# Layer norm of the four plain groups: statistics tile by tile, and ScalarE in place of VectorE for the normalisation

## The chip, the core and the metric

The kernel runs on one core of a Trainium2 chip. A core has TensorE (matrix products, results in PSUM), VectorE, ScalarE and GpSimd (element-wise work), and queues that start DMA transfers. Each engine works through its own queue in order; an instruction that waits for another engine holds up all that stands behind it in its queue. The metric is the time of one execution on the device in microseconds (us).

## What is computed

Two blocks in a row, all in float32. First a linear attention with decay over 4 batches, 8 heads, 768 positions and 64 columns per head, in blocks. Its result x, 4 x 768 x 512, goes through a Fourier mixing block:

```python
X = np.fft.fft(np.fft.fft(x, axis=1), axis=2)
u = x + np.real(X).astype(np.float32)
mu = np.mean(u, axis=-1, keepdims=True)
var = np.mean((u - mu) ** 2, axis=-1, keepdims=True)
un = (u - mu) / np.sqrt(var + 1e-06)
ch = np.maximum(un @ w_ch1, 0.0) @ w_ch2
return u + ch
```

Here w_ch1 is 512 x 2048 and w_ch2 is 2048 x 512. They arrive as float64 and are turned into float32 on the chip (`load_weights`, L203). The change is in the lines of `un`: the mean, the variance and the normalisation.

## The kernel before

**Tiles and groups.** A batch has six tiles of 128 tokens (partitions) by 512 columns. The Fourier transform gives tile t and tile 3 + t together, since the one is the mirror of the other, so a *group* (b, g) is the pair of tiles (g, 3 + g) of batch b, and there are 12 groups, worked through in the order g = 1, 2, 0 of each batch. The first four in that order, (0,1), (0,2), (0,0) and (1,1), are called PLAIN: their MLP is done with ordinary matrix products (`mlp`, L711), beside the attention and the Fourier transforms of the later batches, and fills TensorE while these wait. The other eight, LATE, are written to DRAM and go through a second stage with Strassen-like products (from `late`, L1246), in which fewer multiplications are needed.

**One group in `fft_ln` (L572).** For each t in (1, 2, 0) the width product runs on TensorE (`width`, L605) into one bank of PSUM; ScalarE copies parts of it (L674 to L677); VectorE forms `ds` (L678, L679) and adds it to the two tiles of the group, `u` (L681) and `v_` (L682). For t = 0 one row of `v_` is replaced (L688 to L691). Then `norm(g)` (L622) is called:

- L626 and L627, VectorE: `bn_stats` and `bn_aggr` of each of the two tiles give mean and variance, in `mv`.
- L630 and L631, GpSimd: `ve` = variance + epsilon, `rs` = `ve` to the power -0.5, both tiles in one instruction.
- L644, VectorE: `un` = (x - mean) * power, in two halves per tile, the second half read backwards. `un` has a single buffer (`bufs=1`).
- In a plain group: L649, TensorE transposes the four blocks of `un` into PSUM, and L653, ScalarE copies them into `ut`, which the MLP's first layer reads (L718). In a late group: VectorE transposes in blocks (L657) and the result goes to DRAM (L661).

The plain MLP evicts the first layer's results from three PSUM banks (`pm`) with a Relu on ScalarE, L726, in the second half also on VectorE, L724; its second layer is L732.

**What orders the work.** The Python generators (`weave`, `beside`, `part`) decide in which order instructions are written down, by the costs that they yield (`yield 9.0`, `yield 1.6` and so on). The order of each engine's queue is then fixed at build time by a planner, which plays the program through with its own estimates of durations and puts the earliest-written instruction that it takes to be ready at each engine's turn. So a queue's order is not the program's order, but once built it doesn't change. `tc.keep_in_program_order` pins an instruction behind the one written before it on its engine; the first transpose of the first plain group is pinned in this way. Semaphores between engines are set by the framework.

**GpSimd's queue** also carries the gathers of mirrored rows (L483, L489, L496), and the products `kd` (L304) and state decays (L356) of the attention.

Of the kernel before, what the change touches and what calls it, by code (L numbers as in the profile page):

```python
# [16 lines left out]
AF = mybir.ActivationFunctionType  # L17
ALU = mybir.AluOpType
# [59 lines left out]
def kernel(  # L78
# [10 lines left out]
    nc = tc.nc  # L89
# [14 lines left out]
    G = 2  # L104
    NG = NC // G
    TT = [(t, HC + t) for t in range(HC)]
# [9 lines left out]
    def front_pool(name, bufs):  # L116
        return front_end.enter_context(tc.tile_pool(name=name, bufs=bufs, side="left"))
# [9 lines left out]
    np_ = front_pool("np", 2)  # L127
# [12 lines left out]
    def new(pool, shape, tag, **kw):  # L140
        cnt[0] += 1
        return pool.tile(shape, F32, tag=tag, name=f"{tag}{cnt[0]}", **kw)

    def psum_a(shape):
        return new(pa, shape, "pa")
# [28 lines left out]
    mhalf = const.tile([128, G], F32, name="mhalf")  # L174
# [100 lines left out]
    xs, xn_, xd = {}, {}, {}  # L275
# [224 lines left out]
    def fold_a(b):  # L500
        for a, n in enumerate(BLK):
            yield from fold_x(b, a, n, 1, eo[b][a][1][0:n, 1, 0:DM], xn_[b, HC + a][0:n])
# [69 lines left out]
    def fft_ln(b):  # L572
        sets = []

        def piece(a, i, n):

            c0 = W + QM if i == 4 else QM * (i % 2)
            return sets[a][i in (2, 3)][0:BLK[a], n, c0:c0 + QM]

        if b in LEADS:  # L580
            yield from fold_a(b)
            yield from fold_b(b, sets)
            yield 2.0
        else:
            yield 1.0
            run(fold_a(b))
            yield 6.0 if b - 1 in LEADS else 3.0
            run((folds_apart if b > 1 else fold_b)(b, sets))
            yield 12.0 if b - 1 in LEADS else 9.0


        for i in (0, 1, 4, 2, 3):
            ps = psum_a([128, 2, NK])
            m = 128 if i < 4 else 1
            for n in range(2):
                for a, rows in enumerate(BLK):
                    mm = nc.tensor.matmul(ps[:, n, :], lhsT=piece(a, i, n), rhs=cs[0:rows, a, i in (2, 3), n, :],  # L597
                                          start=(a == 0), stop=(a == 1))
                    if i + n + a == 0:
                        tc.keep_in_program_order(mm)  # L600
            nc.scalar.copy(ys[i][0:m, 0:2 * NK].rearrange("p (k n) -> p n k", n=2), ps[0:m])
            yield 1.4


        def width(t, ps, only_a):  # L605
            y = [ys[i][:, S // 2:S // 2 + 1].broadcast_to([128, 128]) if only_a else ys[i][:, 128 * t:128 * t + 128] for i in range(5)]
            mm = nc.tensor.matmul
            if not only_a:
                mm(ps[:, HM + QM:DM], lhsT=y[2], rhs=dt[:, 2, 0:QM], start=True, stop=True)
            mm(ps[:, HM:HM + QM + 1], lhsT=y[0], rhs=dt[:, 0, :], start=True, stop=False)  # L610
            mm(ps[:, HM:HM + QM + 1], lhsT=y[4], rhs=dt[:, 4, :], start=False, stop=True)
            mm(ps[:, 0:QM], lhsT=y[1], rhs=dt[:, 1, 0:QM], start=True, stop=True)
            if not only_a:
                mm(ps[:, QM:HM], lhsT=y[3], rhs=dt[:, 3, 0:QM], start=True, stop=True)

        def even_odd(t):
            return t.rearrange("p (m r) -> p r m", r=2)

        def halves(t):
            return t.rearrange("p (r k) -> p r k", r=2)  # L620

        def norm(g):  # L622
            mv = new(np_, [128, G, 2], "mv")
            for i in range(G):
                stt = new(np_, [128, 6], "stt")
                nc.vector.bn_stats(stt, xs[b, TT[g][i]])  # L626
                nc.vector.bn_aggr(mv[:, i, :], stt)  # L627
            ve = new(np_, [128, G], "ve")
            rs = new(np_, [128, G], "rs")
            nc.gpsimd.tensor_scalar(ve, mv[:, :, 1], EPS, None, op0=ALU.add)  # L630
            nc.gpsimd.tensor_tensor(rs, ve, mhalf, op=ALU.pow)  # L631

            yield 9.0 if (b, g) == PLAIN[0] else 1.0
            plain = (b, g) in PLAIN
            if plain:
                ut = uts[b, g] = new(up, [128, KO, G * 128], "ut")
            else:

                to = utd[b, g] = dram.tile([128, KO, G * 128], F32, name=f"utd{b}{g}")
            for i in range(G):  # L640
                un = new(np_, [128, DM], "un", bufs=1)
                u = xs[b, TT[g][i]]
                for o, x in ((un[:, 0:HM], u[:, 0:HM]), (un[:, HM:DM], u[:, DM - 1:HM - 1:-1])):
                    nc.vector.tensor_scalar(o, x, mv[:, i, 0:1], rs[:, i:i + 1],  # L644
                                            op0=ALU.subtract, op1=ALU.mult)
                if plain:
                    pt = psum_a([128, KO, 128])
                    for c in range(KO):
                        mm = nc.tensor.transpose(pt[:, c, :], un[:, 128 * c:128 * c + 128], ident)  # L649
                        if (b, g, i, c) == (*PLAIN[0], 0, 0):  # L650

                            tc.keep_in_program_order(mm)
                    nc.scalar.copy(ut[:, :, 128 * i:128 * i + 128], pt)  # L653
                else:

                    uq = new(ep, [128, DM], "e")
                    nc.vector.transpose(uq, un)  # L657
                    for r in range(0, 128, 32):
                        dst = to[:, :, 128 * i + r:128 * i + r + 32].rearrange("(a d) c n -> d c a n", d=32)
                        src = uq[r:r + 32].rearrange("p (c a n) -> p c a n", c=KO, n=32)  # L660
                        nc.sync.dma_start(dst, src)  # L661
                yield 0.7
            if plain:
                return
            for T in TT[g]:
                ud[b, T] = dram.tile([128, DM], F32, name=f"ud{b}{T}")
                nc.sync.dma_start(ud[b, T], xs.pop((b, T)))

        for t in (1, 2, 0):
            ps = psum_a([128, DM])  # L670
            width(t, ps, False)

            A = halves(ps)[:, ::-1, 0:QM]
            nc.scalar.copy(odd[:, 1:HM:2], ps[:, QM:HM])  # L674
            nc.scalar.copy(odd[:, 2:HM:2], ps[:, HM + QM + 1:DM])
            ds = new(fp, [128, 2 * (HM + 2)], "ds")
            nc.scalar.copy(ds[:, HM:2 * HM + 2:HM + 1], ps[:, HM + QM:HM + QM + 1].broadcast_to([128, 2]))  # L677
            nc.vector.tensor_tensor(even_odd(ds[:, 0:HM]), A, even_odd(odd[:, :]), op=ALU.subtract)  # L678
            nc.vector.tensor_tensor(even_odd(ds[:, HM + 1:2 * HM + 1]), A, even_odd(odd[:, :]), op=ALU.add)  # L679
            u, v_ = xs[b, t], xs[b, HC + t]  # L680
            nc.vector.tensor_tensor(halves(u), halves(u), halves(ds)[:, :, 0:HM], op=ALU.add)  # L681
            nc.vector.tensor_tensor(halves(v_), halves(v_), halves(ds[:, 1:DM + 1])[:, ::-1, :], op=ALU.add)  # L682
            yield 1.6
            if t == 0:
                ps = psum_a([128, DM])
                width(HC, ps, True)
                x3 = xn_.pop((b, HC))
                nc.vector.tensor_tensor(even_odd(v_[0:1, 0:HM]), halves(ps[0:1])[:, ::-1, 0:QM],  # L688
                                        even_odd(x3[0:1, 0:HM]), op=ALU.add)
                nc.vector.tensor_tensor(v_[0:1, HM:DM:2], ps[0:1, 0:QM], x3[0:1, HM:DM:2], op=ALU.add)  # L690
                nc.vector.tensor_tensor(v_[0:1, HM + 1:DM:2], ps[0:1, HM + 1:HM + QM + 1],  # L691
                                        x3[0:1, HM + 1:DM:2], op=ALU.add)
                yield 0.9
            yield from norm(t)


    ORDER = [(b, g) for b in range(B) for g in (1, 2, 0)]
    PLAIN, LATE = ORDER[:4], ORDER[4:]
# [565 lines left out]
    def front(b):  # L1264
        yield from attn(b)
        yield from fft_ln(b)
# [15 lines left out]
    def run(gen):  # L1282
        return sum(gen)
# [18 lines left out]
    def beside(lead, t, other, t_other):  # L1302
        return weave(lead, part(other, t_other), t_other / t)

    att1, mix = attn(1), fft_ln(0)
    att0 = attn(0)
    run(part(att0, 2.7))
# [4 lines left out]

    half = [[mlp(b, g, h * FO // 2, (h + 1) * FO // 2) for b, g in PLAIN[:3]] for h in range(2)]
    fr = chain([att1, fft_ln(1)] + [front(b) for b in range(2, B)])
    t_rest, t_back = 3 * t_front - 5 * t_chunk, len(PLAIN) * t_mlp - 50.0
    t_half = 1.5 * t_mlp
# [49 lines left out]
```

## Time and profile before

| | |
|---|---|
| median of 3 runs | 785.93 us (785.44 to 786.23) |
| the profiled execution | 782.96 us |
| its span, first to last instruction | 780.7 us |
| TensorE busy | 756.3 us |
| VectorE busy | 600.9 us |
| ScalarE busy | 231.9 us |
| GpSimd busy | 181.9 us |
| TensorE's granted clock | 1.00 |
| L644, normalisation, 48 instructions | 0.41 us each |
| L631, power, 12 instructions | 0.72 us each |
| first to last transpose of a plain `un` (L649) | 92.4 to 148.4 us |

A line of the profile names the engine (PE is TensorE, PEld its weight loads, DVE VectorE, ACT ScalarE, POOL GpSimd), the line of the kernel, the operation and the tiles as out<-in. Times are counted from the span's start. Behind a line may stand in brackets how long the engine was idle before the instruction and which instruction ended the wait. The span is divided into the attention and Fourier stage with the plain MLP (up to some 391 us), and the second stage, in which TensorE runs the late groups.

### The profile page before, as it was taken

Reading aid. Unit: us, or ns where it says so; the run is one execution under the profiler, and the core shown is the slowest. Engines: PE = TensorE matmul, PEld = TensorE weight load, DVE = VectorE, ACT = ScalarE, POOL = GpSimd, SP = SyncE. Lnnn points to the kernel's source line nnn. Section 1 sums busy time; section 2 is a strip of 40 time slices with the busy share of each in tenths; the row PEclk is TensorE's granted clock in tenths of the full one; section 3 lists DMA queues with packets and bytes.
Section 4 is the critical chain, followed back from the end, with each engine's and each line's share of the span. In section 5 each row is a group of like instructions: output and inputs, shape, how many; then the busy total and the mean of one; then the engine's idle time right before and its main releaser. Section 6 shows DMA issues by size and latency. Waiting matters only on the chain.

```text
span 780.7 us, 14995 instructions
## 1 busy us (share of the span) xinstructions
PE 756.3 (97%) x5784; PEld 646.9 (83%) x5784; DVE 600.9 (77%) x1167; ACT 231.9 (30%) x532; POOL 181.9 (23%) x202
## 2 busy tenths in 40 slices
PE   6989989999999999999999999999999999999997
PEld 5768776858676877858946889999999999999997
DVE  6899889675855585346698999789986699758983
ACT  3765443325531221421101221024311342024310
POOL 3223331010202113211003961360015000230013
PEclk9999999999999999999999999999999999999999
DMA  9979623237852148721243374776545455455442
GB/s 241 255 164 249 189 91 122 87 68 202 221 153 89 55 81 250 194 90 41 55 121 102 140 242 137 264 246 194 181 137 162 142 176 178 133 177 175 137 141 75
DMA packets 152955, 120.21 MB, mean 154 GB/s; under 512 B 114238, under 2 KB 114622, under 8 KB 152886
## 3 DMA queue, kind: packets, MB, share of 16 engines
q1 hardware_dynamic: 145824, 100.51, 45.7%
q0 software_dynamic: 4032, 12.99, 4.6%
q10 hardware_dynamic: 3030, 5.78, 2.0%
q8 instruction: 46, 0.75, 0.4%
q14 instruction: 23, 0.19, 0.1%
HBM read 88.04 MB, written 31.20 MB: 153 GB/s over the span
## 4 chain that ended last, share of the span: by engine, by line
PE 85%; DVE 7%; DMA 4%; ACT 2%; issue 1%; POOL 1%; DVEq 0%; ACTq 0%; POOLq 0%
PE p L1127 22%; PE p L1053 17%; PE pm L732 12%; PE pm L718 11%; PE p L969 6%; PE pa L597 3%; PE pa L332 3%; PE pa L373 3%; PE pa L367 2%; DMA x<-xb,ix 2%; PE pa L308 1%; PE pa L352 1%; PE pa L313 1%; PE pa L389 1%; DVE sc L336 1%
## 5 line engine op out<-in xcount | busy, mean ns | idle before, releaser
L718 PE MATMUL pm<-ut,w 128*128 128x256 f32 x512 | 118.3, 381 | 0.0
L732 PE MATMUL pm<-w,hr 128*128 128x512 f32 x256 | 115.3, 596 | 0.1
L718 PEld LDWEIGHTS pm<-ut,w 128*128 128x128 f32 x512 | 94.5, 190 | 13.6 <-issue 2.1
L732 PEld LDWEIGHTS pm<-w,hr 128*128 128x128 f32 x256 | 46.7, 190 | 50.3 <-issue 48.7
L1148 POOL TENSOR_TENSOR y<-y,u 128x512 f32<-128x512 f32 x12 | 19.9, 1660 | 186.8 <-DVE y L1157 155.6
L1127 PE MATMUL p<-tx,sx 128*128 128x128 f32 x400 | 52.7, 275 | 0.0
L1127 PEld LDWEIGHTS p<-tx,sx 128*128 128x128 f32 x400 | 48.6, 192 | 0.0
L1062 DVE TENSOR_TENSOR ha<-p,ha 128x512 f32<-128x512 f32 x60 | 40.1, 686 | 8.3 <-PE p L1053 8.1
L304 POOL TENSOR_TENSOR kd<-k,decay 128x512 f32<-128x512 f32 x20 | 22.9, 1144 | 96.0 <-PE pa L352 56.1
L1133 ACT COPY y<-p 128x128 f32<-128x128 f32 x48 | 12.7, 265 | 103.6 <-PE p L1127 103.2
L1135 DVE TENSOR_TENSOR y<-p,y 128x128 f32<-128x128 f32 x92 | 25.6, 285 | 16.1 <-PE p L1127 9.4
L1127 PE MATMUL p<-w,ha 128*128 128x128 f32 x288 | 37.4, 275 | 0.0
L336 DVE TENSOR_TENSOR sc<-pa,decay 128x512 f32<-128x512 f32 x48 | 31.5, 683 | 7.6 <-PE pa L332 7.3
L332 PEld LDWEIGHTS pa<-qT,kT 64*128 64x128 f32 x384 | 26.1, 193 | 12.8 <-ACT qT L315 7.6
L1062 DVE TENSOR_TENSOR hs<-p,hs 128x512 f32<-128x512 f32 x39 | 26.2, 686 | 12.3 <-PE p L1053 12.3
L726 ACT ACTIVATE hr<-pm 128x256 f32<-128x256 f32 x44 | 16.7, 384 | 63.9 <-PE pm L718 63.7
L1127 PEld LDWEIGHTS p<-w,ha 128*128 128x128 f32 x288 | 34.9, 192 | 0.1
L1053 PE MATMUL p<-sx,tx 128*128 128x128 f32 x264 | 33.9, 275 | 0.0
L332 PE MATMUL pa<-qT,kT 64*128 64x128 f32 x384 | 30.7, 292 | 3.2 <-ACT qT L315 2.9
L319 DVE TENSOR_TENSOR qs<-pa,qpow 128x512 f32<-128x512 f32 x20 | 13.7, 686 | 24.3 <-ACT qT L315 24.2
L373 PE MATMUL pa<-sc,v 128*64 128x128 f32 x384 | 29.9, 279 | 2.0 <-DVE sc L336 1.9
L1053 PEld LDWEIGHTS p<-sx,tx 128*128 128x128 f32 x264 | 31.6, 192 | 0.0
(267 smaller groups left out, 1731.5 us busy)
## 6 DMA issues: line engine op xcount, KB each, us to landing
tx<-td SPq DMA_DIRECT2D x84, 256.0 KB, 2.7
raw<-in_moe_w_ch_dram SPq DMA_DIRECT2D x32, 512.0 KB, 3.7
tx<-sd SPq DMA_DIRECT2D x63, 256.0 KB, 2.8
k<-in_k_dram SPq DMA_DIRECT2D x24, 256.0 KB, 5.7
q<-in_q_dram SPq DMA_DIRECT2D x24, 256.0 KB, 5.9
v<-in_v_dram SPq DMA_DIRECT2D x24, 256.0 KB, 5.1
td<-tx SPq DMA_DIRECT2D x21, 256.0 KB, 2.0
ud<-x SPq DMA_DIRECT2D x16, 256.0 KB, 2.2
```

The source lines that it names most:

```text
L304: nc.gpsimd.tensor_tensor(kd, kt, kpow, op=ALU.mult)
L332: mm(pss[hi][:, hp, :], lhsT=kT[HD[hi], hp, :], rhs=qT[HD[hi], hp, :], start=True, stop=True)
L336: nc.vector.tensor_tensor(t, pss[hi], decay[:, hi::2, :], op=ALU.mult)
L373: mm(po[HD[hi], hp, :], lhsT=vt[:, 2 * hp + hi, :], rhs=sc[hi][:, hp, :], start=(c == 0 and hp == 0), stop=(hp == HP - 1), skip_group_chec ...
L597: mm = nc.tensor.matmul(ps[:, n, :], lhsT=piece(a, i, n), rhs=cs[0:rows, a, i in (2, 3), n, :], start=(a == 0), stop=(a == 1))
L718: nc.tensor.matmul(ps, lhsT=w1[:, c, 128 * fc:128 * fc + 128], rhs=ut[:, c, :], start=(c == 0), stop=(c == KO - 1))
L732: nc.tensor.matmul(ps, lhsT=hr[(fc - f0) // 4][:, fc % 4, 128 * i:128 * i + 128], rhs=w2[:, fc, :], start=(fc == f0), stop=(fc == f1 - 1))
L969: nc.tensor.matmul(ps, lhsT=s2.A[a][:, kt, 128 * i:128 * i + 128], rhs=U[b][:, kt, :], start=(first and kt == 0), stop=(kt == 1), skip_gro ...
L1053: nc.tensor.matmul(ps[:, 128 * i:128 * i + 128], lhsT=ab[m][0][:, 128 * i:128 * i + 128], rhs=ab[m][1], start=(start and i == 0), stop=Tru ...
L1062: V.tensor_tensor(o, p, o, op=ADD)
L1127: nc.tensor.matmul(ps[:, 0:HM // 2], lhsT=ab[m][0][i], rhs=ab[m][1][:, i, :], start=(start and i == 0), stop=(i == HF // 2 - 1), skip_grou ...
L1135: V.tensor_tensor(o, ps[:, 0:HM // 2], o, op=ADD)
```

## The change

In the plain groups each tile gets statistics of its own. For the first tile `u` they are written down directly behind its sum, ahead of the sum of the second tile; GpSimd's two instructions work on one column instead of two. GpSimd then forms `shift` = mean * power * (-1) for each tile, and ScalarE computes `un` as Identity(power * x + shift), with power and shift as one value per partition, in the same two halves. In the late groups the arithmetic and its order stay as they are.

```diff
-        def norm(g):
-            mv = new(np_, [128, G, 2], "mv")
-            for i in range(G):
+        def statistics(tiles, mv, ve, rs):
+            for i, x in enumerate(tiles):
                 stt = new(np_, [128, 6], "stt")
-                nc.vector.bn_stats(stt, xs[b, TT[g][i]])
+                nc.vector.bn_stats(stt, x)
                 nc.vector.bn_aggr(mv[:, i, :], stt)
-            ve = new(np_, [128, G], "ve")
-            rs = new(np_, [128, G], "rs")
             nc.gpsimd.tensor_scalar(ve, mv[:, :, 1], EPS, None, op0=ALU.add)
-            nc.gpsimd.tensor_tensor(rs, ve, mhalf, op=ALU.pow)
-
+            nc.gpsimd.tensor_tensor(rs, ve, mhalf[:, 0:len(tiles)], op=ALU.pow)
+
+        def norm(g, mv, rs):
             yield 9.0 if (b, g) == PLAIN[0] else 1.0
             plain = (b, g) in PLAIN
...
             for i in range(G):
                 un = new(np_, [128, DM], "un", bufs=1)
                 u = xs[b, TT[g][i]]
+                mean, power = mv[:, i, 0:1], rs[:, i:i + 1]
+                if plain:
+                    shift = new(np_, [128, 1], "shift")
+                    nc.gpsimd.tensor_scalar(shift, mean, power, -1.0, op0=ALU.mult, op1=ALU.mult)
                 for o, x in ((un[:, 0:HM], u[:, 0:HM]), (un[:, HM:DM], u[:, DM - 1:HM - 1:-1])):
-                    nc.vector.tensor_scalar(o, x, mv[:, i, 0:1], rs[:, i:i + 1],
-                                            op0=ALU.subtract, op1=ALU.mult)
+                    if plain:
+                        nc.scalar.activation(o, x, AF.Identity, bias=shift, scale=power)
+                    else:
+                        nc.vector.tensor_scalar(o, x, mean, power, op0=ALU.subtract, op1=ALU.mult)
...
             u, v_ = xs[b, t], xs[b, HC + t]
+            each = (b, t) in PLAIN
+            mv, ve, rs = (new(np_, [128, *n], m) for m, n in (("mv", (G, 2)), ("ve", (G,)), ("rs", (G,))))
             nc.vector.tensor_tensor(halves(u), halves(u), halves(ds)[:, :, 0:HM], op=ALU.add)
+            if each:
+                statistics([u], mv[:, 0:1], ve[:, 0:1], rs[:, 0:1])
             nc.vector.tensor_tensor(halves(v_), halves(v_), halves(ds[:, 1:DM + 1])[:, ::-1, :], op=ALU.add)
...
-            yield from norm(t)
+            if each:
+                statistics([v_], mv[:, 1:2], ve[:, 1:2], rs[:, 1:2])
+            else:
+                statistics([u, v_], mv, ve, rs)
+            yield from norm(t, mv, rs)
```

## The prediction

> **What bounds the kernel now.** I read the page's busy shares first, then the busy time by stretch, then TensorE's waits, then the timeline of one group.
>
> ```profile
> PE 756.3 (97%) x5784; PEld 646.9 (83%) x5784; DVE 600.9 (77%) x1167; ACT 231.9 (30%) x532; POOL 181.9 (23%) x202
> ```
>
> TensorE is busy 97% of 780.7 us. An engine that gets lighter elsewhere buys nothing unless TensorE stops waiting for it. The busy time by stretch (columns: length, then PE, PEld, DVE, ACT, POOL, the clock, DMA) shows where TensorE has gaps in the part that the change touches:
>
> ```profile
> 85.00:90.00 5.00, 4.08 (x52) 3.48 (x54) 5.00 (x13) 2.93 (x6) 1.13 (x2) 1.00 0.59 129
> 90.00:95.00 5.00, 4.15 (x45) 3.23 (x42) 3.32 (x8) 1.66 (x3) 2.56 (x4) 1.00 0.77 210
> 95.00:100.00 5.00, 5.00 (x28) 4.25 (x26) 3.47 (x8) 1.36 (x6) 1.93 (x4) 1.00 0.86 312
> 100.00:105.00 5.00, 3.96 (x31) 3.63 (x31) 3.84 (x10) 3.14 (x7) 0.56 (x1) 1.00 0.04 11
> ...
> 110.00:115.00 5.00, 4.06 (x22) 3.02 (x21) 4.08 (x12) 2.31 (x6) 3.27 (x4) 1.00 0.24 71
> ...
> 145.00:150.00 5.00, 4.06 (x28) 3.33 (x27) 1.55 (x5) 0.42 (x2) 0.94 (x2) 1.00 0.00 0
> ```
>
> The gaps are 0.92, 0.85, 1.04, 0.94 and 0.94 us, 4.7 us in all; from 150 to 345 us the same view has PE busy for the whole of every stretch. The waits of TensorE name what ended them (engine, line, waited for: us in total, times, longest):
>
> ```profile
> PE pa L649 <- DVE un L644: 3.4, 4, 1.0
> PE pa L597 <- DVE fe L520: 1.1, 2, 0.7
> PE pa L367 <- DVE qs L319: 0.6, 1, 0.6
> ```
>
> The first line is the transpose of the normalised tile `un`: four waits, 0.51 at 93.59, 1.04 at 101.16, 0.94 at 113.19 and 0.94 at 146.71. That sum of 3.4 us is all that a quicker `un` can give directly. The timeline of the second group, (b, g) = (0, 2), shows the chain (start, duration, what, and in brackets the idle time before it):
>
> ```profile
> 96.73 0.69 DVE L681 TENSOR_TENSOR x<-x,ds 128x512 f32<-128x512 f32 x1
> 97.34 0.68 DVE L682 TENSOR_TENSOR x<-x,ds 128x512 f32<-128x512 f32 x1
> 97.94 1.28 DVE L626 BATCH_NORM_STATS2 stt<-x 128x6 f32<-128x512 f32 x2
> 99.13 0.30 DVE L627 BATCH_NORM_AGGREGATE mv<-stt 128x2 f32<-128x6 f32 x2
> 99.53 0.22 POOL L630 TENSOR_SCALAR ve<-mv 128x2 f32<-128x2 f32 x1 [2.68 <-DVE mv L627]
> 99.83 0.73 POOL L631 TENSOR_TENSOR rs<-ve,mhalf 128x2 f32<-128x2 f32 x1
> 100.60 0.74 DVE L644 TENSOR_SCALAR un<-x,mv,rs 128x256 f32<-128x256 f32 x2 [1.16 <-POOL rs L631]
> 101.16 0.67 PE L649 MATMUL pa<-ident,un 128*128 128x128 f32 x4 [1.04 <-DVE un L644]
> ```
>
> The reader is to see two things. TensorE's queue reached the transpose about 1 us before `un` was there, and by the same 0.94 to 1.04 us in three groups: the order of its queue was fixed at build time on an estimate of this chain that is some 1 us short. And on VectorE both `bn_stats` run before the first `bn_aggr`, although the program writes stats, aggregate, stats, aggregate: work that is ready goes ahead of work that still waits for its input.
>
> **VectorE: sixteen `tensor_scalar` go.** Each lasts 0.41 us (the row L644), 6.5 us in all; with them go the waits in front of them, 3.2 us for `rs` and 1.6 us for TensorE (four plain groups). Beside: TensorE has MLP matmuls in its queue throughout, and only 0.5 us of its other waits here name VectorE's weight conversion (L228, at 128.75). I take 0; the ends are 0 and -0.5 us.
>
> **ScalarE: sixteen Identity activations come.** No row shows one. The nearest: Relu 128x256 from PSUM 0.384 (L726); SBUF as source against PSUM adds 0.045 for 128x512 (L1067 0.631 against L1060 0.586); a bias from SBUF adds at most 0.04 (L221 0.721 against L219 0.688). That makes 0.43 to 0.5 us for a half, 7 to 8 us in all, on an engine that is busy 30%. Sign, Relu and Copy ran on one table load (1.283 us, at the start); I take it that Identity needs no other, and were it otherwise two swaps per group would cost up to 2.6 us each, which I leave out of the range as very unlikely. The first half of `un` would be ready 0.02 to 0.1 us later than VectorE's, given the same start; I take 0.05.
>
> The Trainium skill ("ScalarE: Activation LUTs", What ACT_TABLE_LOAD costs) adds 93 ns for each [128,1] pointer operand to 186 + 0.833 N ns; two of them at N = 256 make an estimate of 0.585 us, where the row with one pointer shows a good deal less than that addition; by the page the sum below would be 0.1 us higher per group, 0.4 in all. Its rule that plain adds and multiplies belong on VectorE speaks against the change, and no run here shows it for two pointers.
>
> The ScalarE instruction now waits for `shift`. Queued behind it are the Relu evictions L726 that free the three `pm` banks (one per 1.73 us of L718), the copies of `ut`, and the copies L674 to L677 of the next width product. A hold-up of 1 us is less than the 2 x 1.73 us that the other two banks cover: 0.
>
> **GpSimd: two tiny instructions per group become six.** `ve` costs 0.22 (0.58 when VectorE is dense), `rs` 0.72 for two columns; for one column I have only bounds, 0.36 (half) to 0.72. `shift` is like `ve`, 0.22 to 0.58. POOL is 23% busy; the row transfers (L496) of the next batch stand behind them at 112.7 and move by 0.3 to 1 us, behind VectorE work that fills 115 to 137 us: 0.
>
> **The chain to TensorE, group by group.**
> - (0,2) and (1,1). By the order seen on VectorE (a ready instruction first), L682 and both `bn_stats` still run before the first `bn_aggr`, so the tile's own statistics gain 0.13 us (99.30 against 99.43). Then on POOL, with the gaps of the timeline (0.08 between dependent instructions): `ve` of the first tile to 99.61, `ve` of the second to 99.87, `rs` 99.90 to 100.26 or 100.62, `shift` to 100.56 or 100.92, first half of `un` 0.45 later, TensorE 0.15 after it: 101.20 to 101.56, against 101.16 now. If the second tile's `rs` stands ahead of the first's `shift`, 0.36 to 0.72 more, up to 102.28. So +0.04 to +1.1 us for TensorE, if its queue keeps its order. The planner of the queue sees the longer chain too and puts MLP matmuls in front (0.43 us apiece), which takes back about half. I take +0.5 for each of the two, +1.0.
> - (0,0). Here the row-0 repairs L688 to L691 part the tiles: the first `bn_aggr` is at 109.61, the second at 110.93. The first tile's chain starts 1.3 us sooner: `ve` 109.87, `rs` 110.2 to 110.9, `shift` 111.2, `un` 111.7, ready 112.0 where TensorE comes free at 112.25. The wait of 0.94 can go entirely, or stay, if the planner draws the transpose forward by as much. I take -0.7.
> - (0,1). `un` was ready at 92.27, before TensorE (92.49); the new chain has 0.8 us of slack there, since VectorE did other work between `rs` (91.04) and `un` (91.86): 0.
> - Second tiles. `un` has one buffer, so the second tile waits for the first's transposes, as now. On ScalarE the copy of `ut` (0.585) becomes ready at the same moment and may go first: 0.585 + 0.45 + 0.15 = 1.2 us until the next transpose, against 0.86 to 1.03 of matmuls that lie between now. 0 to 0.2 each, 0 to 0.8 in all; against it the 0.51 of (0,1) may go. I take +0.2.
>
> Sum: 0 + 0 + 0 + 1.0 - 0.7 + 0 + 0.2 = **+0.5 us**. From 150 us TensorE is full, so a delay before it reaches the end undiminished. The profiled execution took 782.96 (span 780.7 and 2.3 around it), so it would be 783.5; the runs' median is 785.93, 2.97 above it, and I predict **786.4**.
>
> **The rivals.**
> *Faster*: the four waits of 3.4 us go and nothing takes their place. It needs the first tile's statistics to run ahead of L682, and `shift` right behind its own `rs`. For it: the chain of waits runs through exactly these instructions, and VectorE's queue loses 11 us between 84 and 150. Against: a ready instruction is placed before a dependent one wherever the trace lets me look. -3.4 + 0.4 left = -3.0: 782.9. Chance 0.27.
> *Slower*: GpSimd's queue has the second tile's `rs` ahead of the first's `shift`, and the planner does not know how long `rs` is. For it: `bn_stats` passes `bn_aggr` in this way, and the waits of 1 us show an estimate that is short on this chain. Against: `rs` of the second tile waits for its own `ve`. +1.1 in (0,2) and in (1,1), +0.8 at the second tiles, no gain in (0,0): +3.0, 788.9. It decides from the point where the pair costs over 0.6 us more than planned. Chance 0.36, with a new order of the whole queue after 90 us counted in, which can add about what the gap at 350 to 360 us has now (1.0 us) once more.
> *The change doesn't do what it says*: statistics apart are of no use if both tiles' come out within 0.15 us, as in three of four groups. This is part of my forecast.
>
> **The numbers.** Forecast (within 0.2%, 1.6 us, about what a measurement of this kernel tells from no change): 0.37; faster 0.27; slower 0.36. Range: all four waits gone, 782.5, to the slower rival with a new gap of 1.0, 789.9. I give **782.5 to 789.9**.
>
> **What would show it.** In the changed profile: L649's waits for `un` (now on ACT) near 3.4 us or above means the forecast, under 1 us the faster rival, over 5 us the slower. POOL's order in the group after 96 us decides about `rs` and `shift`. VectorE's order there decides whether statistics came sooner. An activation of over 0.6 us, a second table load, or new gaps of TensorE after 150 us would make the prediction wrong.

## The result, and the profile after

The changed kernel takes 796.60 us (median of 6 runs, 796.09 to 799.46); the kernel before, run beside it, 785.68 us (6 runs, 783.34 to 786.77). The ratio is 1.0151 with an interval of 1.0127 to 1.0175: 1.5% slower, outside the range of the prediction. The profiled execution took 796.48 us, with a span of 794.7, 14.0 us longer than the span before; the medians differ by 10.9, since the profiled execution before lies 2.7 us under its median here.

The busy times of the changed kernel:

```profile
PE 761.0 (96%) x5784; PEld 651.4 (82%) x5784; DVE 597.5 (75%) x1151; ACT 239.1 (30%) x548; POOL 186.4 (23%) x218
```

VectorE and ScalarE moved as the diff says (16 instructions fewer, 16 more). TensorE runs the same 5784 instructions, yet is busy 4.7 us longer. The waits of TensorE, then ScalarE, then VectorE (engine, tile and line, what ended the wait: us in total, times, longest). In the changed kernel `un` of a plain group is L647, its transpose L653, `shift` L644:

```profile
PE pa L653 <- ACT un L647: 11.8, 4, 5.4
```

```profile
ACT un L647 <- POOL shift L644: 14.3, 4, 5.6
```

```profile
DVE e L223 <- ACT e L221: 14.8, 5, 6.7
```

TensorE's waits for `un` grew from 3.4 to 11.8 us. With +8.4 of waits and +4.7 of busy time, 13.1 of the 14.0 us are named. Some 1.0 us of the 14.0 is there ahead of the plain groups: the products of L367 that begin at 83.87 us before begin at 84.88, and up to there the engines run the same instructions in the same order in both kernels, so it isn't the change's. Of the four waits for `un`, three (3.33, 5.41 and 1.84 us) end with ScalarE's own wait for GpSimd's `shift`. The fourth, 1.17 us at the second tile of (0,1), does not: there ScalarE was still at the copies of L376 and L657 when the buffer of `un` came free. In the kernel before, VectorE had this row in the stretch of 84 to 165 us:

```profile
DVE un L644 <- POOL rs L631: 4.1, 4, 1.2
```

Three of these four stops, 3.2 us, are in plain groups; the last, 0.84 us at 157.16, is in the late group (1,2), whose code is as before. After the change VectorE never stops for GpSimd in a plain group. Where it waits most now, it is for ScalarE's weight conversion (L221), which stands in ScalarE's queue behind the `un` that waits.

The timeline of the changed kernel's third group, (0,0), is where the largest wait lies (start, duration, what, in brackets the idle time before it):

```profile
117.38 4.71 POOL L644 TENSOR_SCALAR shift<-mv,rs 128x1 f32<-128x1 f32 x1
117.39 0.16 DVE L626 BATCH_NORM_AGGREGATE mv<-stt 128x2 f32<-128x6 f32 x1
117.48 0.65 DVE L470 TENSOR_TENSOR fe<-fo,xn 65x512 f32<-65x512 f32 x1
118.06 0.41 DVE L223 TENSOR_TENSOR e<-e 128x512 bf16<-128x512 bf16 x1
...
120.94 0.41 DVE L220 TENSOR_SCALAR e<-raw 128x512 uint16<-128x512 uint16 x1
121.27 0.67 DVE L227 SCALAR_TENSOR_TENSOR w<-raw,w 128x512 f32<-128x512 uint32 x1
122.12 0.60 ACT L647 ACTIVATE un<-x,shift,rs 128x256 f32<-128x256 f32 x1 [5.63 <-POOL shift L644]
...
122.77 0.69 PE L653 MATMUL pa<-ident,un 128*128 128x128 f32 x2 [5.41 <-ACT un L647]
```

The reader is to see that one instruction on 128 numbers takes 4.71 us, that VectorE works without a gap all that time (six more VectorE instructions stand where lines are left out, each starting before the one ahead of it has drained), and that `shift` ends at 122.09, 0.15 us after VectorE's last instruction (121.27 + 0.67 = 121.94) has ended and its queue paused. ScalarE, which waits for `shift`, starts 0.03 us behind that, so a second engine bears out the end of this long instruction. The group (0,2) shows the same in small:

```profile
101.55 0.72 POOL L627 TENSOR_SCALAR ve<-mv 128x1 f32<-128x1 f32 x1 [3.79 <-DVE mv L626]
...
102.36 1.32 POOL L628 TENSOR_TENSOR rs<-ve,mhalf 128x1 f32<-128x1 f32 x1
...
103.76 0.68 POOL L627 TENSOR_SCALAR ve<-mv 128x1 f32<-128x1 f32 x1
104.53 0.57 POOL L628 TENSOR_TENSOR rs<-ve,mhalf 128x1 f32<-128x1 f32 x1
105.08 0.51 POOL L644 TENSOR_SCALAR shift<-mv,rs 128x1 f32<-128x1 f32 x2
...
106.05 1.18 PE L653 MATMUL pa<-ident,un 128*128 128x128 f32 x4 [3.33 <-ACT un L647]
```

The first three GpSimd instructions, beside VectorE's weight conversion (101.51 to 104.36), are stretched; the later ones, when VectorE has nothing to do, last 0.57 and 0.26 each. It also shows GpSimd's order: the second tile's `ve` and `rs` stand ahead of the first tile's `shift`.

Last, the busy time of the changed kernel by stretch, around and behind the waits that end at 106.05, 122.77 and 159.59 (columns: length, PE, PEld, DVE, ACT, POOL, the granted clock, DMA):

```profile
106.00:108.00 2.00, 1.95 (x7) 1.57 (x8) 0.00 (x0) 1.78 (x4) 0.00 (x0) 0.50 0.04 8
...
120.00:122.00 2.00, 0.00 (x0) 0.00 (x0) 1.95 (x5) 0.00 (x0) 2.00 (x1) 1.00 0.00 0
122.00:124.00 2.00, 1.23 (x4) 1.14 (x5) 0.00 (x0) 1.63 (x4) 1.14 (x4) 0.70 0.01 4
124.00:126.00 2.00, 2.00 (x7) 1.53 (x7) 0.00 (x0) 0.76 (x2) 0.43 (x1) 0.50 0.35 131
...
160.00:162.00 2.00, 1.95 (x7) 1.52 (x7) 0.00 (x0) 1.38 (x4) 0.00 (x0) 0.58 0.00 0
```

Behind each of the three waits (3.33, 5.41 and 1.84 us) the clock is half for some 3.4 us. Half of 3.4 is lost, three times: 5.1 us, about the 4.7 by which TensorE is busier. So the changed kernel pays for a long wait twice.

### The profile page after: what moved, and what is told of

It is laid out like the page before. It is cut to its first block, busy times and chain, and to the rows that moved or that the text cites. A ratio compares the mean times of both kernels' runs of the same rounds, so it can differ in the third digit from the quotient of the medians.

```text
span 794.7 us, 15023 instructions
## 1 busy us (share of the span) xinstructions
PE 761.0 (96%) x5784; PEld 651.4 (82%) x5784; DVE 597.5 (75%) x1151; ACT 239.1 (30%) x548; POOL 186.4 (23%) x218
## 4 chain that ended last, share of the span: by engine, by line
PE 66%; POOL 5%; issue 5%; DMA 2%; DVE 1%; SPq 0%; ACT 0%; POOLq 0%; DVEq 0%
PE p L1139 17%; PE p L1065 17%; PE pm L744 12%; PE pm L730 11%; POOL tx L817 3%; PE pa L332 2%; PE pa L597 2%; PE pa L373 1%; PE pa L367 1%; DMA ur<-utd 1%; PE pa L352 1%; PE pa L308 1%; PE pa L389 1%; PE pa L313 1%; POOL w L813 1%
## 5 line engine op out<-in xcount | busy, mean ns | idle before, releaser
L730 PE MATMUL pm<-ut,w 128*128 128x256 f32 x512 | 121.5, 388 | 0.0
L730 PEld LDWEIGHTS pm<-ut,w 128*128 128x128 f32 x512 | 96.7, 195 | 13.8 <-issue 1.6
L336 DVE TENSOR_TENSOR sc<-pa,decay 128x512 f32<-128x512 f32 x48 | 31.3, 682 | 7.9 <-PE pa L332 7.6
L627 POOL TENSOR_SCALAR ve<-mv 128x1 f32<-128x1 f32 (+1 forms) x16 | 5.2, 328 | 124.7 <-DVE mv L626 124.4
L223 DVE TENSOR_TENSOR e<-e 128x512 bf16<-128x512 bf16 x32 | 15.0, 467 | 23.9 <-ACT e L221 20.8
L319 DVE TENSOR_TENSOR qs<-pa,qpow 128x512 f32<-128x512 f32 x20 | 13.7, 686 | 24.8 <-ACT qT L315 24.7
```

What stands on the lines that cost most here:

```text
L336: nc.vector.tensor_tensor(t, pss[hi], decay[:, hi::2, :], op=ALU.mult)
L730: nc.tensor.matmul(ps, lhsT=w1[:, c, 128 * fc:128 * fc + 128], rhs=ut[:, c, :], start=(c == 0), stop=(c == KO - 1))
```

## The experiments

Three theories were on the table. **Starvation**: GpSimd gets nowhere while VectorE works without a stop; before, VectorE's own wait for `rs` made the pause in which GpSimd finished, and the change took that pause away. **Longer chain**: six instructions on GpSimd in place of two, and the second tile's in front of the first's `shift`, are simply longer. **ScalarE**: its halves are slower and its queue holds others up. Diffs are against the changed kernel. The median of the kernel before, run beside them, was 783.8 to 783.9 us; what a ratio is worth in us is worked out from it (a ratio of 1.0108 is 8.5 us).

### Statistics apart, VectorE normalises as before

```diff
-                if plain:
-                    shift = new(np_, [128, 1], "shift")
-                    nc.gpsimd.tensor_scalar(shift, mean, power, -1.0, op0=ALU.mult, op1=ALU.mult)
...
-                    if plain:
-                        nc.scalar.activation(o, x, AF.Identity, bias=shift, scale=power)
-                    else:
-                        nc.vector.tensor_scalar(o, x, mean, power, op0=ALU.subtract, op1=ALU.mult)
+                    nc.vector.tensor_scalar(o, x, mean, power, op0=ALU.subtract, op1=ALU.mult)
```

> The tiles' statistics apart as in the change, but VectorE normalises and there is no shift. Theory S (GpSimd is starved while VectorE runs SBUF instructions without a stop; before, VectorE stopped at the normalisation and waited for the power): VectorE stops there again, no GpSimd instruction of the statistics lasts over 0.8 us in the plain groups, TensorE waits 3 to 6 us for un, 784 to 788 us. Theory C (the chain on GpSimd is simply longer, six instructions for two, and two powers one after the other): two powers of 0.57 stand in the chain in place of one of 0.72, about 1 us more in three groups, 787 to 790 us.

Measured: 784.49 us, ratio 1.0001 (0.9988 to 1.0015). The waits for `un` are a little below what was expected:

```profile
PE pa L647 <- DVE un L643: 2.7, 5, 0.8
```

Four instructions on GpSimd in place of two, with the second tile's in front, cost nothing that can be measured: `rs` of one column lasts 0.57, `ve` at most 0.30. So the first half of the change is neutral by itself, and nothing is lost without the second. The next run has the second half alone.

### Joint statistics as before, ScalarE normalises

```diff
+            if plain:
+                shifts = new(np_, [128, G], "shift")
+                nc.gpsimd.tensor_tensor(shifts, mv[:, :, 0], rs, op=ALU.mult)
+                nc.gpsimd.tensor_scalar(shifts, shifts, -1.0, None, op0=ALU.mult)
...
-                    shift = new(np_, [128, 1], "shift")
-                    nc.gpsimd.tensor_scalar(shift, mean, power, -1.0, op0=ALU.mult, op1=ALU.mult)
+                    shift = shifts[:, i:i + 1]
...
-            each = (b, t) in PLAIN
+            each = False
```

> Both tiles' statistics together as before, but ScalarE normalises, with one shift for both tiles (two tiny GpSimd instructions per group behind the power). Theory S: VectorE doesn't stop, the GpSimd instructions are stretched to several us in at least one group, TensorE waits over 8 us for un, 792 to 798 us. Theory C: the chain is 0.5 us of shift and 0.2 us of a slower activation longer than before, 787 to 790 us, and no GpSimd instruction of it lasts over 0.8 us.

Measured: 793.01 us, ratio 1.0108 (1.0073 to 1.0143), waits for `un` 8.1 us. GpSimd's queue in the group (0,0) of this kernel:

```profile
117.83 2.52 POOL L627 TENSOR_SCALAR ve<-mv 128x2 f32<-128x2 f32 x1 [11.44 <-ACT hr L741]
120.43 1.14 POOL L628 TENSOR_TENSOR rs<-ve,mhalf 128x2 f32<-128x2 f32 x1
```

So the second half alone costs 8.5 of the 11.8 us; the rest comes only with both halves together. Here it is `ve`, an instruction that the kernel before has too, that lasts 2.52 us in place of 0.58. It ends at 120.35, beside the first pause of VectorE in that stretch (120.26 to 120.30). In these kernels `shift`, `ve` and `rs` are each hit in turn, according to where VectorE's run begins.

### VectorE copies each shift, and ScalarE reads the copy

```diff
                     nc.gpsimd.tensor_scalar(shift, mean, power, -1.0, op0=ALU.mult, op1=ALU.mult)
+                    held = new(np_, [128, 1], "held")
+                    nc.vector.tensor_copy(held, shift)
...
-                        nc.scalar.activation(o, x, AF.Identity, bias=shift, scale=power)
+                        nc.scalar.activation(o, x, AF.Identity, bias=held, scale=power)
```

> The changed kernel, with one thing added: VectorE copies each shift (128x1) and ScalarE takes its bias from the copy, so VectorE has to stop and wait for GpSimd, and the chain has one hop more. Theory S: with VectorE held GpSimd is free, shift takes 0.3 us in place of 4.7, TensorE's waits for un fall below 7 us, 787 to 791 us. Theory C: one hop more per tile makes it as slow as the changed kernel or slower, 796.5 to 798 us.

Measured: 789.18 us, ratio 1.0054 (1.0031 to 1.0077), waits for `un` 5.9 us. No GpSimd instruction of the chain lasts over 0.72 us. An instruction, a wait and a hop more made the kernel some 7 us quicker. But the copy also lies in the chain, so a cleaner form follows.

### The same copy, read by nobody, in all plain groups and in (0,0) alone

```diff
                     nc.gpsimd.tensor_scalar(shift, mean, power, -1.0, op0=ALU.mult, op1=ALU.mult)
+                    held = new(np_, [128, 1], "held")
+                    nc.vector.tensor_copy(held, shift)
```

> The changed kernel, and VectorE copies each shift once it is there, but nobody reads the copy: ScalarE takes its bias from shift itself. So VectorE stops for GpSimd in each plain group and gives nothing to the chain. If GpSimd is starved while VectorE runs on without a stop, the time is that of the run in which ScalarE read the copy (789.2), or up to 1 us less since the hop is gone: 788 to 790; no GpSimd instruction of the chain above 0.8 us, TensorE's waits for un 5 to 6 us. If the loss lies in the longer chain or in ScalarE alone, a further instruction and a wait on VectorE can only cost: 796 to 799, un waits 11 to 13 us.

Measured: 787.81 us (12 runs), ratio 1.0049 (1.0035 to 1.0064). The group (0,0) of this kernel, and the two waits that count:

```profile
115.30 0.26 POOL L644 TENSOR_SCALAR shift<-mv,rs 128x1 f32<-128x1 f32 x1
115.60 0.15 DVE L646 COPY held<-shift 128x1 f32<-128x1 f32 x1 [0.99 <-POOL shift L644]
115.60 0.60 ACT L649 ACTIVATE un<-x,shift,rs 128x256 f32<-128x256 f32 x1 [0.71 <-POOL shift L644]
...
116.26 0.44 PE L655 MATMUL pa<-ident,un 128*128 128x128 f32 x2 [0.49 <-ACT un L649]
```

```profile
DVE held L646 <- POOL shift L644: 6.3, 4, 2.1
```

```profile
PE pa L655 <- ACT un L649: 4.9, 4, 1.6
```

The same `shift` lasts 0.26 us in place of 4.71, and TensorE waits 0.49 in place of 5.41, because VectorE stood still for 0.99 us. Of the 1.51% that the change costs, 1.02 (some 8 us) are gone by copies whose result is thrown away (5.8 to 10.2 us by the two intervals). The copies do nothing but make VectorE wait 6.3 us. One rival is that the planner gave the queues another order for the added instructions. The traces speak against it: from 80 to 130 us TensorE, VectorE, ScalarE and GpSimd run the same instructions in the same order in both kernels, apart from the copies. Behind that, up to 400 us, two instructions of the weight conversion on VectorE have changed places, and two products on TensorE stand further ahead.

With the same copy in the group (0,0) alone (`if (b, g) == (0, 0):` ahead of it):

> As the run before, but VectorE copies the shift (unread) in the group (0,0) alone. If the starvation is a matter of the place where VectorE runs on, the shift of 4.7 us there becomes 0.3 to 0.7, TensorE's wait of 5.4 us there some 1 to 1.5, and the half clock behind it stays or goes: 4 us gained, up to 6 with the clock, 790.5 to 793; the waits in (0,2) and (1,1) stay 3.3 and 1.8. If it is not, 796 to 798 with the 5.4 still there.

Measured: 790.78 us, ratio 1.0070 (1.0044 to 1.0097). The wait in (0,0) is 0.32 us (expected were 1 to 1.5), `shift` there 0.26; in (0,2) TensorE still waits 3.33 us behind an `rs` of 1.31. So the starvation is where VectorE runs on, and that one place costs 1.0151 - 1.0070 = 0.8%, some 6 us (3.6 to 9.2 by the two intervals), with the clock.

### ScalarE forms the shift, VectorE is not held

VectorE writes -mean behind the statistics, and ScalarE multiplies it with the power, so GpSimd has only `ve` and `rs` left.

```diff
-                    nc.gpsimd.tensor_scalar(shift, mean, power, -1.0, op0=ALU.mult, op1=ALU.mult)
+                    nc.scalar.activation(shift, minus[:, i:i + 1], AF.Identity, scale=power)
```

> The changed kernel with the shift taken off GpSimd: VectorE forms -mean (128x1, right behind the statistics, waiting for nothing), ScalarE multiplies it by the power. VectorE isn't held. Theory S: the shift of 4.7 us is gone, but the power can still be stretched, TensorE waits 5 to 9 us for un, 789 to 794 us. Theory C: a GpSimd instruction of 0.27 us is exchanged for one of 0.2 to 0.3 us on ScalarE, 795 to 797 us.

Measured: 789.78 us, ratio 1.0060 (1.0041 to 1.0079), waits for `un` 6.8 us. GpSimd in the group (0,0) of this kernel:

```profile
117.52 2.58 POOL L627 TENSOR_SCALAR ve<-mv 128x1 f32<-128x1 f32 x1 [0.68 <-DVE mv L626]
```

GpSimd has one instruction per tile less here, and the kernel loses less, but the second tile's `ve` is still starved.

### The whole GpSimd chain, but VectorE normalises

VectorE computes power * x + shift, with all six GpSimd instructions as in the change.

```diff
-                        nc.scalar.activation(o, x, AF.Identity, bias=shift, scale=power)
+                        nc.vector.tensor_scalar(o, x, power, shift, op0=ALU.mult, op1=ALU.add)
```

> The changed kernel with all six GpSimd instructions per group, but VectorE computes un = power * x + shift in place of ScalarE. It asks what is left of the loss once VectorE is held (the kernel with the held VectorE was 0.5% over before). Theory P (GpSimd's longer chain is the rest): as slow as with the held VectorE, 787.5 to 790 us, TensorE's waits for un 5 to 6 us. Theory A (ScalarE is the rest: halves of 0.6 us in place of 0.41, behind the copies of ut and oT in its queue): 784 to 787 us, waits of 3 to 4.5 us. In both, no GpSimd instruction of the chain lasts over 0.8 us.

Measured: 787.46 us, ratio 1.0044 (1.0016 to 1.0072), waits for `un` 5.1 us (0.57, 1.97, 0.67, 1.90). VectorE waits 6.0 us for `shift`, and GpSimd's instructions last at most 0.72 us. So without starvation and without ScalarE the longer chain costs some 3 us; the interval (1.3 to 5.6 us) doesn't fix that closely. Its two waits of 1.97 and 1.90 us, which end at 101.94 and 150.08, are followed by a drop of the clock (columns as above, the clock third from the end):

```profile
104.00:108.00 4.00, 4.00 (x23) 3.92 (x22) 3.40 (x9) 2.86 (x8) 0.00 (x0) 0.68 0.38 131
...
152.00:156.00 4.00, 4.00 (x21) 3.75 (x20) 0.47 (x2) 1.00 (x4) 0.00 (x0) 0.71 0.00 0
```

### VectorE forms the shift, ScalarE normalises

```diff
-                    nc.gpsimd.tensor_scalar(shift, mean, power, -1.0, op0=ALU.mult, op1=ALU.mult)
+                    nc.vector.tensor_scalar(shift, mean, power, -1.0, op0=ALU.mult, op1=ALU.mult)
```

> The changed kernel with the shift formed by VectorE instead of GpSimd. VectorE has to stop and wait for the power, GpSimd has four instructions in place of six, ScalarE normalises as in the change. Theory P: most of the rest of the loss goes with the two shifts, 785 to 787 us. Theory A: the rest stays, 787.5 to 789.5 us, and the second tile of the first group still waits 1.2 us. Theory S alone asks only that no GpSimd instruction of the chain lasts over 0.8 us.

Measured: 786.18 us, ratio 1.0022 (1.0005 to 1.0039).

```profile
PE pa L653 <- ACT un L647: 3.4, 5, 1.2
```

Now VectorE stops for `rs` (4.6 us in all), GpSimd's instructions last at most 0.58, the clock doesn't drop in the plain groups, and 1.7 us (0.4 to 3.1) are left. What they are is not shown. ScalarE's slower halves and the hop are candidates, but TensorE's waits for `un` are 3.4 us in all, as in the kernel before. One of them is ScalarE's: 1.17 us at the second tile of (0,1), where the kernel before has 0.51. All versions in which ScalarE normalises have that 1.17. This is the form in which the idea of the change costs next to nothing; it gains nothing either.

### The shift directly behind its own power

The two `shift` instructions are moved into the statistics, each directly behind its `rs`, so that GpSimd takes them in that order where its queue allows.

```diff
                 statistics([u], mv[:, 0:1], ve[:, 0:1], rs[:, 0:1])
+                nc.gpsimd.tensor_scalar(shifts[:, 0:1], mv[:, 0, 0:1], rs[:, 0:1], -1.0, op0=ALU.mult, op1=ALU.mult)
```

> The changed kernel with the shift written down behind the power of its own tile, so that in the second and fourth group GpSimd has the first tile's shift ahead of the second tile's power. The slower rival of the prediction (the second tile's power ahead of the first's shift) asks for 0.6 us less of waits in each of the two groups, 1 to 2 us in all: 794.5 to 795.5 us. Theory S: VectorE still runs without a stop, GpSimd instructions of over 1 us stay, though perhaps others than now; 793 to 798 us, no systematic gain.

Measured: 795.35 us, ratio 1.0130 (1.0100 to 1.0160). The waits in (0,2) and (1,1) fall by 0.55 (3.33 to 2.78) and 0.54 (1.84 to 1.30); the one in (0,0) stays 5.41, and behind it:

```profile
118.72 4.70 POOL L689 TENSOR_SCALAR shift<-mv,rs 128x1 f32<-128x1 f32 x1
```

So the order that my slower rival named costs about 1.1 us of the 11.8. The rest was not the order.

### A second buffer for the normalised tile

As the first experiment, and the second tile's `un` lies in another buffer, so that it need not wait for the first tile's transposes.

```diff
-                un = new(np_, [128, DM], "un", bufs=1)
+                un = new(ep, [128, DM], "e") if plain and i else new(np_, [128, DM], "un", bufs=1)
```

> The kernel with statistics apart and VectorE normalising, in which the second tile's un has a buffer of its own (one of the two that the weight conversion uses). VectorE needn't wait for the first tile's transposes (three waits of 0.5 to 0.6 us before). If VectorE's time mattered here, 782 to 783.5 us; if only TensorE's waits matter, 783 to 785 us, as without it. The buffer could hold up a weight conversion; then slower by up to 2 us.

Measured: 783.70 us, ratio 0.9993 (0.9979 to 1.0007); waits 1.7 + 1.3 us, against 2.7 with one buffer. Nothing gained that can be measured: the waits are spread over both tiles and are no shorter. No version tried is measurably quicker than the kernel before.

## Why the prediction was wrong, step by step

- **VectorE: "sixteen `tensor_scalar` go", taken at 0.** This is the step that failed. I counted the waits that vanish on VectorE as time that nobody needs, and looked only for who might gain. Who lost was GpSimd: VectorE's wait for `rs` was the pause in which `ve` and `rs` ran. The copies that nobody reads put the pause back, and some 8 us of the 12 are gone.
- **GpSimd: `shift` "0.22 to 0.58".** It lasted 0.26 where VectorE paused and 4.71 where it didn't; in the changed kernel `rs` went to 1.32, and `ve` to 2.58 in the run where ScalarE forms the shift. My bound 0.58 "when VectorE is dense" came from a row (0.58 at 111.18) whose dense stretch ended with VectorE waiting for that very GpSimd chain; a second row (0.57 at 89.66) stood beside one weight conversion, behind which came products read from PSUM (L336). The trace before held a warning, on a row of GpSimd that I priced at nothing, beside VectorE work that "fills 115 to 137 us":

```profile
114.11 6.41 POOL L496 DMA_INDIRECT x<-xb,ix  x1 [0.30 <-issue]
```

  The same instruction at 112.72, when VectorE had just waited and was at `un`, took 1.08. The long one ended at 120.52, while VectorE ran on to 122.73, so it warns of a slowdown without showing what ends it.
- **"A hold-up of 1 us" of ScalarE, 0.** The hold-up was up to 5.63 us, and VectorE waited 14.8 us in five waits for the weight conversion behind it. That is a consequence, not the cause: with the unread copies these waits fall to 3.0 us.
- **ScalarE's half "0.43 to 0.5".** It takes 0.60 (the median of 16 is 0.599), and the two halves of a tile together 1.09. The nearest row here was no substitute for a price with two pointers. The estimate of 0.585 from the figures of the Trainium skill ("ScalarE: Activation LUTs", What ACT_TABLE_LOAD costs) agrees with the trace within 0.02 us. By it the sum had been 0.4 us higher, so this error is small. No further table load came.
- **Clock: not in the sum at all.** I read 1.00 in all of the stretches before and did not ask from which wait on that changes. TensorE's 4.7 us of added busy time are a third of the loss in the profiled execution. That the drops follow the waits is read from the rows; no run takes the clock by itself.
- **(0,0): -0.7.** I expected its wait to go. It grew from 0.94 to 5.41, the largest single term. With the unread copies it is 0.49, less than before, so the step was right but for the starvation.
- **(0,2) and (1,1): +0.5 each.** Their waits grew by 2.3 (1.04 to 3.33) and 0.9 (0.94 to 1.84). With the unread copies they are 1.63 and 1.65, that is 0.6 and 0.7 more than before, so without starvation this term was nearly right.
- **The slower rival.** Its order on GpSimd came true in (0,2) and (1,1), and TensorE's waits passed its mark of 5 us, but its mechanism is about 1.1 us of 11.8. What decided was not in any rival.
- **What held.** Statistics apart gain nothing (ratio 1.0001). TensorE takes a delay before 150 us to the end undiminished: the run of 64 products of the MLP's second layer that began at 391.30 us begins at 405.30, the whole 14.0 later. The second tile of (0,1) waits as foreseen, since the copy of `ut` goes first (1.17 us, 0.51 before). The longer GpSimd chain alone costs 3.4 us (1.3 to 5.6), near the slower rival's 3.0 and above the forecast's 0.5.

The account by ratios, in us of 784: the change +11.8; with VectorE held by unread copies +3.8; the chain alone, VectorE normalising, +3.4; ScalarE alone, VectorE forming the shift, +1.7; statistics alone +0.1. The intervals of the three in the middle overlap, so how the last 4 us divide between chain, ScalarE and clock stays open; that some 8 belong to the starvation, with the clock behind it, doesn't.

## What to carry to other kernels

A wait of VectorE for GpSimd is no idle time to be won back: ahead of taking it away, look for what GpSimd has to do in that moment and what VectorE will run instead. Here it was work from SBUF to SBUF that starved GpSimd. If a short GpSimd chain lies on the critical path, let VectorE consume its result, or keep the chain off GpSimd. And where TensorE is full, a wait of 2 us or a little less can cost up to 1.7 us more than itself by the half clock behind it (half of the 3.4 us seen here); it does so in some cases and not in others.

## What the runs showed of the hardware

- **GpSimd stands still beside an unbroken run of VectorE on SBUF.** One 128x1 `tensor_scalar`: 0.26 us free, 4.71 beside eleven VectorE instructions in a row, done 0.15 after the last. None of the ten boundaries between them let it in. All eleven read and write SBUF. An unbroken VectorE is not enough: in the group (0,1) of the same kernel VectorE has no pause from 89.06 to 93.45 either, but there L319 and L336 take their first input from PSUM (`pa`), with one instruction on SBUF between them (L227, 91.00 to 91.65), and GpSimd keeps its pace:

```profile
90.33 0.65 DVE L319 TENSOR_TENSOR qs<-pa,qpow 128x512 f32<-128x512 f32 x1
...
90.82 0.58 POOL L628 TENSOR_TENSOR rs<-ve,mhalf 128x1 f32<-128x1 f32 x1
...
91.50 0.28 POOL L644 TENSOR_SCALAR shift<-mv,rs 128x1 f32<-128x1 f32 x1
91.57 1.28 DVE L336 TENSOR_TENSOR sc<-pa,decay 128x512 f32<-128x512 f32 x2
```

  That the input from PSUM makes the difference fits these rows; no run tries it alone. Beside a `bn_stats` GpSimd was not stretched either (`rs` 0.57 at 116.71, with `bn_stats` at 116.47 to 117.15). The Trainium skill ("GPSIMD Engine Reference", 1. Specifications) says that the two share their interfaces to SBUF and lists a VectorE instruction with two SBUF inputs, or in a faster two-port mode, as what collides; "SBUF — State Buffer" (SBUF: two separate sides) describes an exclusive lock held for one instruction. The runs agree with both as to what collides, the rows from PSUM included. But if a lock came free behind each VectorE instruction and GpSimd needed it once, it would have cost one such instruction, at most 0.7 us, where the trace shows 4.7; why GpSimd gets no turn in between is not shown here.
- **Half clock after less than 2 us, but not each time.** The Trainium skill ("TensorE: Matmul & The Clock Gate", What's actually happening) puts the drop behind an idle window of some 3.4 us. The runs show it behind single waits of 1.84, 1.88, 1.90 and 1.97 us, in the run with the unread copies behind one of 1.65 (ending at 152.59), and not behind one of 2.13 (at 107.07, joint statistics), 1.63 (at 105.69, unread copies) or 1.64 and 1.67 (ScalarE forming the shift). A wait of 1.84 does both: in the changed kernel the clock falls behind it, and where ScalarE reads the copy it doesn't:

```profile
154.85 0.44 PE L655 MATMUL pa<-ident,un 128*128 128x128 f32 x2 [1.84 <-ACT un L649]
```

```profile
156.00:160.00 4.00, 4.00 (x26) 3.50 (x25) 0.76 (x2) 3.08 (x8) 0.00 (x0) 1.00 0.32 110
```

  So no run here gives a threshold. The stay at half clock, some 3.4 us, agrees.
- **The drop isn't the same in each execution.** With the copy in (0,0) alone, the three runs with a mean clock of 0.992 to 0.994 have spans of 789.8 to 790.9 us, the three with 0.996 to 0.997 have 785.4 to 788.2. A loss by the clock therefore needs several runs to be sized.
